# Score products split 512 + 128 and 384 + 256 over the halves of TensorE's rows, in four PSUM banks

## The chip, the cores and the metric

The kernel runs on one core of a Trainium2 chip. The core has TensorE (PE, with its weight loads as PEld), VectorE (DVE), ScalarE (ACT), GpSimd (POOL) and SyncE (SP, which here issues the DMAs). Matmuls write PSUM, which has eight banks of 512 fp32 columns by 128 partitions; VectorE and ScalarE read them from there. The metric is the device time of one execution in microseconds, as the median of several runs.

## The reference

The input x has 2048 rows of 576. One half of the work is causal attention over segments of 512 rows with 32 heads of 18 columns, together with a memory that is carried over the segments. The other is a feed-forward net with a gate over 4608 hidden columns. A gate per row mixes both.

```python
for s in range(N):                       # N = 4 segments of L = 512 rows
    qs, ks, vs = q[:, :, s], k[:, :, s], v[:, :, s]
    logits = jnp.einsum("bhqd,bhkd->bhqk", qs, ks) * scale + mask
    p = _softmax(logits, axis=-1)
    a_dot = jnp.einsum("bhqk,bhkd->bhqd", p, vs)
    ...
    o = g * a_mem + (1.0 - g) * a_dot
...
b = (_gelu(x @ w_gate) * (x @ w_up)) @ w_down
return g * a + (1 - g) * b
```

## The kernel before

Products are made of fp16 pairs (a high and a low part), so that a product of two fp32 operands takes three matmuls. After a first stage (projections, memory; about 230 us) the kernel runs 72 steps, `step(v)`, each of which forms the hidden columns of the feed-forward net for one tile of 128 hidden columns and half of the rows. Into most steps two further kinds of work are woven: the attention of one head for two segments, and the down products of the block of hidden columns before. The last stage multiplies by the output weights.

Four engines (PE, ACT, DVE, POOL) run their instructions in the order in which the code emits them; this order is written out by hand in `step`. SyncE's queue is not held to it.

**The row halves.** A head has 18 columns. Its queries and keys lie as three parts of 18 (54 rows), once at partitions 0 to 53 and once, copied, at partitions 64 to 117. So a score product takes 54 of the 128 rows of TensorE and can use either half of them. In `scores(a)` a segment of a head has four score products, one for each block of 128 queries (`qi` 0 to 3); causality leaves (qi + 1) x 128 key columns. `PIECES` says at which partition (0 or 64) each one reads, and in which order they are issued. Before, 512 columns (qi 3) are at 0, 384 and 128 (qi 2 and 0) at 64 in one bank, and 256 (qi 1) at 0.

**The banks.** `bank(tag, bufs)` takes one of the PSUM buffers of a tag. Tags G, U, V and pv have one bank each, st and dn two, which are taken in turn. The down chains take dn: `down` runs six matmuls (L999) and one VectorE instruction that adds the result to `acc` (L1007, in the first block L1005). Here dn is also taken by the score product of 256 columns, the others take st. Once in four steps a sum for the scales takes a dn bank as well.

**The evictions.** `scores` gives back a function `piece(i)`; `put(a, i)` calls it in a later place. It makes VectorE read a score bank, add the mask and write the logits to `pf` with their maximum (L910, a custom instruction and one that reads the accumulator).

**A step**, with k = v - 2 the head: `end_pair` finishes the hidden columns of the step before (`hidden`, L1021: VectorE scales what lies in G and U). The matmuls of this step fill V, G and U (L1039, L1046), with copies between them on VectorE (L1141, L1144, L1176). Between them stand single down chains (`early`, five a step). Then come `low_rests` (L1051, two matmuls of 64 rows), `scores(2k)` (the middle group), the additions of Y and V to the tiles g1 and g0 on VectorE (L1195, L1203; Y is the tile of bank U, X that of G), the values products of a segment before (`values`, L954, bank pv), two more chains, the last product into U, three chains (`late`), `low_rests` again, and `scores(2k + 1)` (the end group). The next step's first matmul goes to V. Segment 2k is evicted within the step, segment 2k + 1 at the start of the next. In one step of four, VectorE writes the result of four heads (`result_low`, L983) between the late chains' additions.

Of the kernel before, what the change touches and what calls it, by code (L numbers as in the profile page):

```python
# [13 lines left out]
OP = mybir.AluOpType  # L14
# [4 lines left out]
P = 128  # L19
# [3 lines left out]
DH = 18  # L23
L = 512
# [18 lines left out]
def kernel(ctx: ExitStack, tc: tile.TileContext, xs, wqk, wv, wo, wgu, wd, beta, out):  # L43
    nc = tc.nc
    pe, act, dve, pool, sp = nc.tensor, nc.scalar, nc.vector, nc.gpsimd, nc.sync
# [6 lines left out]
    def bank(tag, bufs=1, dt=F32):  # L52
        return ps.tile([P, 512 if dt == F32 else 1024], dt, name=tag, tag=tag, bufs=bufs)
# [255 lines left out]
    def low_d(f):  # L309
        t = pair_d[f]  # L310
        pool.tensor_tensor(t[:, 1], raw_d.pop(f), t[:, 0], OP.subtract)  # L311
# [67 lines left out]
    mask = cst.tile([P, L], BF16, name="mask")  # L379
# [16 lines left out]
    with tc.tile_pool(name="prj", bufs=2, side="right", reuse_waits="tile") as pp:  # L396
# [204 lines left out]
        with tc.manual_schedule(engines=ORDERED):  # L601
# [3 lines left out]
            start = bank("G")  # L605
# [241 lines left out]
    with tc.tile_pool(name="keep", bufs=2, side="right", reuse_waits="tile") as kp, ExitStack() as tail:  # L847
        home.update(d=kp)
        turns.update(of=2)
        hp, qts, kts, vts, obs, mx, prob = {}, {}, {}, {}, {}, {}, {}  # L850
# [34 lines left out]

        COL = [0, P, 3 * P, 6 * P, 10 * P]

        PIECES = (((3,), 0), ((2, 0), 64), ((1,), 0))

        def scores(a):  # L890

            k, e = divmod(a, 2)
            q, kt = qts[k], kts[k]
            mx[a] = ap_.tile([P, 4], F32, name="mx", bufs=2)
            prob[a] = ap_.tile([P, 10 * P], F32, name="pf", bufs=2)
            put = []
            for qis, r in PIECES:
                o = bank("dn", 2) if qis == (1,) else bank("st", 2)
                spots, off, h = [], 0, slice(r, r + 3 * DH)
                for qi in qis:  # L900
                    n = (qi + 1) * P
                    pe.matmul(o[:, off : off + n], q[h, e * L + qi * P : e * L + (qi + 1) * P],  # L902
                              kt[h, e * L : e * L + n], start=True, stop=True)
                    spots.append((qi, o[:, off : off + n]))
                    off += n
                put.append(spots)

            def piece(i):
                for qi, ov in put[i]:
                    dve.tensor_tensor_reduce(prob[a][:, COL[qi] : COL[qi + 1]], ov, mask[:, L - (qi + 1) * P :],  # L910
                                             1.0, -3e38, OP.add, OP.max, mx[a][:, qi : qi + 1])

            return piece

# [103 lines left out]
        def hidden(f, c, o, t):  # L1018

            sc = scl[f // 2][0]  # L1020
            dve.scalar_tensor_tensor(t, o, sc[:, 6 + c : 7 + c], t, OP.mult, OP.mult)  # L1021

        def hidden_pair(f, c, t):
            hh = hp[f, c] = (kp if f % 2 else mp2).tile([P, 2, L], F16, name=f"hh{f % 2}", bufs=6 - 2 * (f % 2))
            act.activation(hh[:, 0], t, AF.Copy)  # L1025
            pool.tensor_tensor(hh[:, 1], t, hh[:, 0], OP.subtract)  # L1026

        def gelu(f, c, o, t):
            act.activation(t, o, AF.Gelu_apprx_tanh, scale=scl[f // 2][0][:, 2 + c : 3 + c])  # L1029
# [77 lines left out]

        ends, puts = [], {}

        def end_pair():  # L1110

            for g in ends:
                hidden(*g)
            for f, c, o, g in ends:
                hidden_pair(f, c, g)
            ends.clear()

        def step(v):
# [3 lines left out]
            c, e = 2 * p, 2 * p + 1  # L1122
            k = v - LAG
# [4 lines left out]
            put = lambda a, i: puts[a](i) if a in puts else None  # L1128

            done = (k - 5) // 4 if i4 == 3 and 0 <= (k - 5) // 4 < H // 2 else None  # L1130
            low = (k - 6) // 4 if i4 == 0 and 0 <= (k - 6) // 4 < H // 2 - 1 else None
            x1, x2_, t = x16[c], x16[e], xt[p]
            end_pair()
            if v == 3:
                high_g(2, 1)
                low_g(2, 1)
# [11 lines left out]
                scale_result()  # L1148
            some(fb - 1, early[:1])
            put(2 * k - 1, 1)  # L1150
            put(2 * k - 1, 2)
            puts.pop(2 * k - 1, None)
            if on(k - 2):
                values(2 * k - 3)
# [37 lines left out]
                low_rests(f, (V, G4, x1), (Y, G4, x2_))  # L1192
            if on(k):
                puts[2 * k] = scores(2 * k)
            dve.tensor_tensor(g1, Y, g1, OP.add)  # L1195
            gelu(f, e, g1, g1)
            if v == 3:
                for n in range(2):
                    high_d(n)
                    low_d(n)  # L1200
            put(2 * k, 2)
            if fb:
                dve.tensor_tensor(g0, V, g0, OP.add)  # L1203
                gelu(f, c, g0, g0)
# [32 lines left out]
            if on(k):  # L1237
                puts[2 * k + 1] = scores(2 * k + 1)
# [37 lines left out]
        with tc.manual_schedule(engines=ORDERED):  # L1276
            for v in range(2 * NF):
                step(v)

                if v == LAST:  # L1280
                    atn.close()
                    op_ = tail.enter_context(tc.tile_pool(name="outp", bufs=2, side="right", reuse_waits="tile"))
                if v >= LAST:
                    turned(2 * (v - LAST))
                    turned(2 * (v - LAST) + 1)
                    finish(v - LAST)
            end_pair()
            turns.update(of=3)


            fb = NB - 1
            for t in range(10, 16):
                turned(t)
            for t in range(16):
                for n in range(2):
                    down(fb, t, n)
                for n in range(2):
                    o = bank("st", 2)
                    chain_x(o[:, :NH], lambda i: ot[t][:, i], lambda k, b: wos[k][:, b, n * NH : (n + 1) * NH])
                    av = acc[:, t, n * NH : (n + 1) * NH]  # L1300
                    dve.scalar_tensor_tensor(av, o[:, :NH], gate[:, 2, t : t + 1], av, OP.mult, OP.add)
                    if t == 15:
                        sp.dma_start(out[t * P :, n * NH : (n + 1) * NH], av)
                if t < 15:
                    sp.dma_start(out[t * P : (t + 1) * P, :], acc[:, t])
# [40 lines left out]
```

## Time and profile before

| | |
|---|---|
| median of 3 runs | 1612.19 us (1610.37 to 1613.04) |
| span of the profiled execution | 1608.8 us, granted TensorE clock 1.000 |
| the same execution outside its span | not listed; median less span is 3.4 us |
| DMA q1 | 206.92 MB, 71.1% of 16 engines |
| score products (L902) | 512 of 11924 matmuls, 259.3 to 1420.1 us |
| down products (L999) | 3396 matmuls into dn listed, 476.8 us, 286 ns each |
| score evictions (L910) from st | 183.9 us in 384 |
| additions of down products (L1007) | 274.0 us in 534, 516 ns each |

A row of the timeline gives start and length in us, engine, line, operation, what is written and read, tile shape and count; in brackets stands how long the engine was idle before and who ended that. Rows of equal instructions that follow each other are merged. The recorded length of a matmul is from its start to its modelled end, so matmuls overlap in the list. A row of groups gives the count, then busy us and mean ns of one, then the idle time before. A row of windows gives the stretch, its length, and for each engine busy us and count, then the granted clock, the DMA share and GB/s.

### The profile page before, as it was taken

What the parts mean: (1) busy time and instruction counts of PE and PEld (TensorE: products, weight loads), DVE (VectorE), ACT (ScalarE), POOL (GpSimd) and SP (SyncE); (2) the same over time, 40 slices, a digit from 0 to 9 for tenths busy, and PEclk for the clock granted to TensorE, in tenths of its full rate; (3) what the DMA queues carried; (4) which work ended last, traced back from release to release, by engine and by line L of the source; (5) the groups of instructions that cost most, each with busy time, mean ns of one, the idle gap of its engine ahead of it and who ended that gap; (6) DMA issues with size and microseconds to landing.
All of it is one profiled execution on the core that took longest, in us unless ns stands there. A gap on an engine that the chain in (4) does not pass through costs nothing.

```text
span 1608.8 us, 32608 instructions
## 1 busy us (share of the span) xinstructions
PE 1594.9 (99%) x11924; PEld 933.3 (58%) x11924; DVE 1141.2 (71%) x2938; ACT 1162.3 (72%) x1968; POOL 1132.9 (70%) x1093
## 2 busy tenths in 40 slices
PE   9999999999999999999999999999999999999999
PEld 6655754555555555555555555555555555555577
DVE  6575785677777777777777777777777777765543
ACT  6666446888888888888888888888888888863200
POOL 2233647798978888888978788887879787885200
PEclk9999999999999999999999999999999999999999
DMA  6532343788878788888987898878788797837251
GB/s 243 190 122 81 133 146 85 122 139 126 136 122 141 123 142 125 142 136 126 141 128 136 126 145 124 145 123 155 130 132 135 130 136 129 129 65 166 49 133 60
DMA packets 472016, 209.00 MB, mean 130 GB/s; under 512 B 427568, under 2 KB 437040, under 8 KB 471344
## 3 DMA queue, kind: packets, MB, share of 16 engines
q1 hardware_dynamic: 471856, 206.92, 71.1%
q8 instruction: 94, 1.54, 0.4%
q14 instruction: 66, 0.54, 0.1%
HBM read 90.99 MB, written 27.26 MB: 73 GB/s over the span
## 4 chain that ended last, share of the span: by engine, by line
PE 96%; DMA 1%; DVE 1%; POOL 1%; ACT 0%; issue 0%; SPq 0%; POOLq 0%; DVEq 0%
PE dn L999 26%; PE U L1039 17%; PE V L1039 12%; PE G L1039 11%; PE pv L954 4%; PE st L328 3%; PE st L318 3%; PE dn L328 2%; PE G L318 2%; PE U L1046 2%; PE st L902 2%; PE V L1051 1%; PE U L318 1%; PE G L1051 1%; PE V L1046 1%; PE G L1046 1%
## 5 line engine op out<-in xcount | busy, mean ns | idle before, releaser
L934 POOL TENSOR_TENSOR ph<-pf,ph 128x512 f16<-128x512 f32 (+1 forms) x256 | 354.0, 1404 | 177.8 <-ACT ph L933 175.9
L999 PE MATMUL dn<-paird,hh 128*128 128x288 f16 x3396 | 476.8, 286 | 0.9 <-POOL paird L311 0.9
L1039 PEld LDWEIGHTS <-pairg 128*128 128x128 f16 x3024 | 285.0, 98 | 312.6 <-issue 17.6
L999 PEld LDWEIGHTS <-hh 128*128 128x128 f16 x3456 | 332.3, 98 | 138.1 <-issue 2.6
L1007 DVE SCALAR_TENSOR_TENSOR acc<-dn,ev,acc 128x288 f32<-128x288 f32 x534 | 274.0, 516 | 95.9 <-PE dn L999 87.2
L923 ACT ACTIVATE pf<-pf,mb,esc 128x512 f32<-128x512 f32 (+3 forms) x512 | 292.9, 642 | 6.7
L1039 PE MATMUL G<-x,pairg 128*128 128x512 f16 x864 | 209.9, 379 | 4.0 <-DVE gl L1021 4.0
L1039 PE MATMUL U<-xt,pairg 128*128 128x512 f16 x864 | 210.0, 379 | 0.0
L1026 POOL TENSOR_TENSOR hh<-gl,hh 128x512 f16<-128x512 f32 x144 | 163.9, 1159 | 56.1 <-ACT hh L1025 56.1
L910 DVE CUSTOM_DVE_ANT_0 pf<-st,mask 128x512 f32<-128x512 f32 (+2 forms) x384 | 183.9, 504 | 0.0
L299 POOL TENSOR_TENSOR pairg<-raw,pairg 128x640 f16<-128x640 f32 (+2 forms) x144 | 173.9, 1230 | 10.6 <-ACT pairg L295 10.6
L933 ACT ACTIVATE ph<-pf 128x512 f16<-128x512 f32 (+1 forms) x256 | 172.4, 720 | 0.0
L1176 DVE COPY gl<-U 128x512 f32<-128x512 f32 x72 | 49.8, 691 | 135.6 <-PE U L1039 135.6
L295 ACT ACTIVATE pairg<-raw 128x640 f16<-128x640 f32 (+2 forms) x144 | 89.5, 648 | 69.9 <-POOL raw L289 40.7
L264 POOL TENSOR_SCALAR raw<-raw,sc 128x640 f32<-128x640 f32 x72 | 134.8, 1885 | 0.0
L1029 ACT ACTIVATE gl<-gl,sc 128x512 f32<-128x512 f32 x144 | 98.3, 717 | 45.9 <-DVE gl L1195 25.5
L1039 PE MATMUL V<-xt,pairg 128*128 128x512 f16 x432 | 105.7, 381 | 0.0
L1195 DVE TENSOR_TENSOR gl<-U,gl 128x512 f32<-128x512 f32 x72 | 49.7, 690 | 78.6 <-PE U L1051 71.3
L1039 PE MATMUL U<-x,pairg 128*128 128x512 f16 x432 | 105.0, 379 | 0.4 <-DVE gl L1195 0.4
L1039 PE MATMUL V<-x,pairg 128*128 128x512 f16 x432 | 104.8, 378 | 0.4 <-ACT hh L1025 0.2
L1025 ACT ACTIVATE hh<-gl 128x512 f16<-128x512 f32 x144 | 82.8, 616 | 24.9 <-DVE gl L1021 24.8
L920 ACT ACTIVATE mb<-mx,esc 128x4 f32<-128x4 f32 x128 | 37.8, 295 | 86.5 <-DVE mx L910 83.7
(268 smaller groups left out, 2566.6 us busy)
## 6 DMA issues: line engine op xcount, KB each, us to landing
raw<-in_wgu_dram SPq DMA_DIRECT2D x36, 640.0 KB
rawd<-in_wd_dram SPq DMA_DIRECT2D x36, 288.0 KB
qk<-stage SPq DMA_DIRECT2D x36, 256.0 KB
qt<-qk SPq DMA_DIRECT2D x128, 72.0 KB
kt<-qk SPq DMA_DIRECT2D x128, 72.0 KB
vp<-vstage SPq DMA_DIRECT2D x16, 296.0 KB
vt<-vp SPq DMA_DIRECT2D x16, 296.0 KB
qt<-qk SPq DMA_DIRECT2D x128, 36.0 KB
```

What stands on the lines that cost most here:

```text
L264: pool.tensor_scalar(r, r, scl[f // 2][0][:, 0:1], None, OP.mult)
L299: pool.tensor_tensor(spot(f, *p, 1), raw_g[f][:, p[0] : p[1]], spot(f, *p, 0), OP.subtract)
L318: pe.matmul(o, w(k, a), x[:, 4 * b + k], start=n == 0, stop=False)
L910: dve.tensor_tensor_reduce(prob[a][:, COL[qi] : COL[qi + 1]], ov, mask[:, L - (qi + 1) * P :], 1.0, -3e38, OP.add, OP.max, mx[a][:, qi : q ...
L923: act.activation(r, r, AF.Exp, bias=b[:, qi : qi + 1], scale=esc[:, 0, c : c + 1])
L933: act.activation(h[:, 0, cols], p[:, cols], AF.Copy)
L934: pool.tensor_tensor(h[:, 1, cols], p[:, cols], h[:, 0, cols], OP.subtract)
L999: pe.matmul(o[:, :NH], hh[:, a, q * P : (q + 1) * P], w[:, b, n * NH : (n + 1) * NH], start=i == 0, stop=i == 5)
L1007: dve.scalar_tensor_tensor(av, o[:, :NH], ev, av, OP.mult, OP.add)
L1026: pool.tensor_tensor(hh[:, 1], t, hh[:, 0], OP.subtract)
L1029: act.activation(t, o, AF.Gelu_apprx_tanh, scale=scl[f // 2][0][:, 2 + c : 3 + c])
L1039: pe.matmul(o, w[:, i, (a + k) * P : (a + k + 1) * P], x[:, b + k], start=start and k == 0 and i == 0 and b == h, stop=k == 1 and i == 1, ...
```

## The change

The four products are issued as 512 columns at partition 0, 384 at 64, 256 at 64 and 128 at 0. Each has a bank of its own: the first two in st, the last two in dn. `piece(i)` evicts one product. The two in dn are evicted first: for segment 2k directly behind the scores, ahead of the addition into g1; for segment 2k + 1 in the next step's `end_pair`, behind the scaling of G and ahead of that of U.

```diff
-        PIECES = (((3,), 0), ((2, 0), 64), ((1,), 0))
+        PIECES = ((3, 0), (2, 64), (1, 64), (0, 0))
...
-            for qis, r in PIECES:
-                o = bank("dn", 2) if qis == (1,) else bank("st", 2)
-                spots, off, h = [], 0, slice(r, r + 3 * DH)
-                for qi in qis:
-                    n = (qi + 1) * P
-                    pe.matmul(o[:, off : off + n], q[h, e * L + qi * P : e * L + (qi + 1) * P],
-                              kt[h, e * L : e * L + n], start=True, stop=True)
-                    spots.append((qi, o[:, off : off + n]))
-                    off += n
-                put.append(spots)
+            for i, (qi, r) in enumerate(PIECES):
+                h, n = slice(r, r + 3 * DH), (qi + 1) * P
+                o = bank("st" if i < 2 else "dn", 2)[:, :n]
+                pe.matmul(o, q[h, e * L + qi * P : e * L + (qi + 1) * P], kt[h, e * L : e * L + n],
+                          start=True, stop=True)
+                put.append((qi, o))
...
-        def end_pair():
+        def end_pair(between=()):
-            for g in ends:
+            for i, g in enumerate(ends):
                 hidden(*g)
+                if i == 0:
+                    for put in between:
+                        put()
...
-            end_pair()
+            end_pair([lambda i=i: put(2 * k - 1, i) for i in (2, 3)])
...
             put(2 * k - 1, 1)
-            put(2 * k - 1, 2)
...
                 puts[2 * k] = scores(2 * k)
+            put(2 * k, 2)
+            put(2 * k, 3)
             dve.tensor_tensor(g1, Y, g1, OP.add)
             gelu(f, e, g1, g1)
...
-            put(2 * k, 2)
```

The lines of the changed kernel stand up to five lower in number: the scores are L900 there, their evictions L906, the down chains L995, their additions L1003, `hidden` is L1017 and the next step's first product L1035.

TensorE at the end of a step, behind the late chains: the scores and the first matmul of the next step. Before, and then now, with the semaphores of the engines that each waits for:

```order
L902 LDWEIGHTS qt
L902 MATMUL st<-kt,qt 128x512
L902 LDWEIGHTS qt
L902 MATMUL st<-kt,qt 128x384
L902 LDWEIGHTS qt
L902 MATMUL st<-kt,qt 128x128
L902 LDWEIGHTS qt
L902 MATMUL dn<-kt,qt 128x256 [waits DVE_49]
L1039 LDWEIGHTS pairg
L1039 MATMUL V<-xt_2147,pairg 128x512
```

```order
L900 LDWEIGHTS qt
L900 MATMUL st<-kt,qt 128x512
L900 LDWEIGHTS qt
L900 MATMUL st<-kt,qt 128x384
L900 LDWEIGHTS qt
L900 MATMUL dn<-kt,qt 128x256 [waits DVE_49]
L900 LDWEIGHTS qt
L900 MATMUL dn<-kt,qt 128x128 [waits DVE_49]
L1035 LDWEIGHTS pairg
L1035 MATMUL V<-xt_2147,pairg 128x512
```

The product of 128 columns has moved to the end and into dn, and two of the four now wait for VectorE, where one did.

VectorE at the same place, from the additions of the late chains into the next step (ISA is the eviction of a score, first the custom instruction and then the reading of its accumulator). Before, and then now:

```order
L1007 SCALAR_TENSOR_TENSOR acc<-dn,ev,acc 128x288 [waits PE_49] x2
L1021 SCALAR_TENSOR_TENSOR gl<-G,sc,gl 128x512 [waits PE_49,Activation_49]
L1021 SCALAR_TENSOR_TENSOR gl<-U,sc,gl 128x512 [waits PE_49]
L1141 COPY gl<-V 128x512 [waits PE_49,Pool_49]
L910 ISA pf,mx<-st,mask 128x512 [waits Pool_49]
```

```order
L1003 SCALAR_TENSOR_TENSOR acc<-dn,ev,acc 128x288 [waits PE_49] x3
L1017 SCALAR_TENSOR_TENSOR gl<-G,sc,gl 128x512 [waits PE_49,Activation_49]
L906 ISA pf,mx<-dn,mask 128x256 [waits PE_49,Pool_49]
L906 ISA mx 128x1
L906 ISA pf,mx<-dn,mask 128x128 [waits PE_49]
L906 ISA mx 128x1
L1017 SCALAR_TENSOR_TENSOR gl<-U,sc,gl 128x512
L1140 COPY gl<-V 128x512 [waits PE_49]
L906 ISA pf,mx<-st,mask 128x512
```

The two evictions from dn have come between the scalings of G and U. (The first list is from a step in which L983 stands between the additions, so it shows two of three.)

VectorE in the middle of a step, from the addition of the last chain before the scores. Before, and then now:

```order
L1007 SCALAR_TENSOR_TENSOR acc<-dn,ev,acc 128x288 [waits PE_49]
L1195 TENSOR_TENSOR gl<-U,gl 128x512 [waits PE_49]
L910 ISA pf,mx<-dn,mask 128x256 [waits PE_49]
L910 ISA mx 128x1
L1203 TENSOR_TENSOR gl<-V,gl 128x512
```

```order
L1003 SCALAR_TENSOR_TENSOR acc<-dn,ev,acc 128x288 [waits PE_49]
L906 ISA pf,mx<-dn,mask 128x256 [waits PE_49]
L906 ISA mx 128x1
L906 ISA pf,mx<-dn,mask 128x128 [waits PE_49]
L906 ISA mx 128x1
L1195 TENSOR_TENSOR gl<-U,gl 128x512
L1202 TENSOR_TENSOR gl<-V,gl 128x512
```

Both evictions from dn now stand ahead of the addition of U.

More of the change, by code (lines that the diff above doesn't have):

```diff
@@ L896, in scores @@
             put = []
-            for qis, r in PIECES:
-                o = bank("dn", 2) if qis == (1,) else bank("st", 2)
-                spots, off, h = [], 0, slice(r, r + 3 * DH)
-                for qi in qis:
-                    n = (qi + 1) * P
-                    pe.matmul(o[:, off : off + n], q[h, e * L + qi * P : e * L + (qi + 1) * P],
-                              kt[h, e * L : e * L + n], start=True, stop=True)
-                    spots.append((qi, o[:, off : off + n]))
-                    off += n
-                put.append(spots)
+            for i, (qi, r) in enumerate(PIECES):
[4 more added lines that the diff above has]
+                put.append((qi, o))
             def piece(i):
-                for qi, ov in put[i]:
-                    dve.tensor_tensor_reduce(prob[a][:, COL[qi] : COL[qi + 1]], ov, mask[:, L - (qi + 1) * P :],
-                                             1.0, -3e38, OP.add, OP.max, mx[a][:, qi : qi + 1])
+                qi, ov = put[i]
+                dve.tensor_tensor_reduce(prob[a][:, COL[qi] : COL[qi + 1]], ov, mask[:, L - (qi + 1) * P :],
+                                         1.0, -3e38, OP.add, OP.max, mx[a][:, qi : qi + 1])
             return piece
```

## The prediction, on record before the changed kernel ran

> **What bounds the kernel now.** I read the page's busy times first, then the chain of work that ended last, then the busy times of one long stretch, and after that the timeline of TensorE and VectorE around a few score products.
>
> ```profile
> span 1608.8 us, 32608 instructions
> PE 1594.9 (99%) x11924; PEld 933.3 (58%) x11924; DVE 1141.2 (71%) x2938; ACT 1162.3 (72%) x1968; POOL 1132.9 (70%) x1093
> PE 96%; DMA 1%; DVE 1%; POOL 1%; ACT 0%; issue 0%; SPq 0%; POOLq 0%; DVEq 0%
> 300.00:1420.00 1120.00, 1120.00 (x8929) 639.71 (x8929) 845.58 (x2305) 942.09 (x1570) 940.71 (x866) 1.00 0.84 133
> ```
>
> The last row is the stretch in which the scores are computed: TensorE is busy for 1120.00 of 1120.00 us at a granted clock of 1.00, and VectorE for 845.58. So there TensorE's own sequence sets the time. What makes it shorter is gained and what makes it wait is lost, unless it waits already; the other engines matter only through the banks and tiles that they release.
>
> A step has two groups of four score products. The one in its middle, around 806.4:
>
> ```profile
> 806.16 0.39 PE L1051 MATMUL U<-x,pairg 64*128 64x512 f16 x1
> 806.38 0.38 PE L902 MATMUL st<-kt,qt 54*128 54x512 f16 x3
> 806.55 0.21 PE L902 MATMUL st<-kt,qt 54*128 54x128 f16 x1
> 806.60 0.27 PE L902 MATMUL dn<-kt,qt 54*128 54x256 f16 x1
> 806.80 0.67 PE L954 MATMUL pv<-vt,pt 128*128 128x37 f16 x20
> 807.32 0.65 PE L999 MATMUL dn<-paird,hh 128*128 128x288 f16 x4
> 806.59 0.69 DVE L1195 TENSOR_TENSOR gl<-U,gl 128x512 f32<-128x512 f32 x1 [1.32 <-PE U L1051]
> 807.20 0.41 DVE L910 CUSTOM_DVE_ANT_0 pf<-dn,mask 128x256 f32<-128x256 f32 x1
> 807.54 0.08 DVE L910 DVE_READ_ACCUMULATOR2_ANT mx<- 128x1 f32 x1
> L902 PE MATMUL st<-kt,qt 54*128 54x512 f16 x128 | 48.4, 378 | 0.0
> L902 PE MATMUL st<-kt,qt 54*128 54x384 f16 x128 | 41.5, 324 | 0.0
> L902 PE MATMUL dn<-kt,qt 54*128 54x256 f16 x128 | 34.2, 267 | 0.0
> L902 PE MATMUL st<-kt,qt 54*128 54x128 f16 x128 | 27.3, 213 | 0.0
> ```
>
> The row at 806.38 holds three products: 512 and 384 columns start together, on different halves of the rows, and 128 columns at 806.55, when the second half is through with its 384. The 256 columns start at 806.60, when the first half is through with its 512. The last four rows give the streaming time: 128 columns more cost 54 to 57 ns, so a product streams for about 55 ns for each 128 columns, and some 158 ns of its recorded time are the way through the array. The halves now stream 768 and 512 columns. From the start of the last product (806.60) to the next full-row matmul (806.80) are 0.20 us: 0.11 of streaming and 0.09 in which nothing starts.
>
> **Part 1: the even halves.** Afterwards the second half streams 384 and 256 columns, the first 512 and 128: 640 each. The 256 start at +0.17 (after the group's start) and have streamed at 0.28, the 128 start at +0.22 and have streamed at 0.275. Before, the last column was through at 0.33. That is **0.05 us less a group**, 128 groups, 6.4 us, if nothing waits. This part changes no weight load or eviction in number, and two evictions of one tile become evictions of two.
>
> **Part 2: the fourth product needs a second down bank.** The two dn banks are taken in turn by the down chains and the scores, so two score products in a row take both, and the second takes the bank that the last chain before it has just filled. At the end of a step three chains stand directly before the scores. The first and the last end group of the usual kind, each with the last chain's eviction, the last score product and the next step's first matmul (the last one's score product started at 1420.11 in the same way):
>
> ```profile
> 297.75 0.52 DVE L1005 TENSOR_SCALAR acc<-dn,ev 128x288 f32<-128x288 f32 x1 [0.25 <-PE dn L999]
> 298.09 0.27 PE L902 MATMUL dn<-kt,qt 54*128 54x256 f16 x1
> 298.29 0.39 PE L1039 MATMUL V<-xt,pairg 128*128 128x512 f16 x1
> 1419.77 0.52 DVE L1007 SCALAR_TENSOR_TENSOR acc<-dn,ev,acc 128x288 f32<-128x288 f32 x1 [0.25 <-PE dn L999]
> 1420.31 0.39 PE L1039 MATMUL V<-xt,pairg 128*128 128x512 f16 x1
> ```
>
> The last chain's eviction ends at 298.27, and the score product on dn started at 298.09, while that eviction ran: it had the other bank. Its successor in the turn gets the bank that is not free before 298.27. The fourth product now waits for that, on TensorE in order, with the whole next step queued behind it. How long TensorE takes to follow VectorE stands in a wait of the later part:
>
> ```profile
> 1510.72 0.74 DVE L1021 SCALAR_TENSOR_TENSOR gl<-G,sc,gl 128x512 f32<-128x512 f32 x1
> 1511.52 0.38 PE L1039 MATMUL G<-x,pairg 128*128 128x512 f16 x1 [1.00 <-DVE gl L1021]
> ```
>
> The first ends at 1511.46, the second starts 0.05 later. So the fourth starts at 298.32, has streamed at 298.375, and with the same 0.09 the next step starts at 298.47 instead of 298.29: **+0.18**. The gap of 0.09 I take as it stands, because it stands behind every group whatever its last product; its bounds are nothing, if the next weights are loaded during the wait, and 0.18, if the waiting group pays a change of rows twice.
>
> In one step of four, VectorE writes a head group's result (L983) between the evictions, and they end later. First and last of these:
>
> ```profile
> L983 DVE SCALAR_TENSOR_TENSOR oh<-ob,wsc,oh x16: 807/809/810, 370.3 to 1455.5; 128x576 f16<-128x576 f32 x16
> 370.98 0.93 DVE L1007 SCALAR_TENSOR_TENSOR acc<-dn,ev,acc 128x288 f32<-128x288 f32 x2
> 371.86 0.39 PE L1039 MATMUL V<-xt,pairg 128*128 128x512 f16 x1
> 1400.94 0.93 DVE L1007 SCALAR_TENSOR_TENSOR acc<-dn,ev,acc 128x288 f32<-128x288 f32 x2
> 1401.83 0.39 PE L1039 MATMUL V<-xt,pairg 128*128 128x512 f16 x1
> ```
>
> Evictions end at 371.91; plus 0.05, 0.055 and 0.09 is 372.11 against 371.86: **+0.25**. Of the sixteen results one (1455.5) comes after the last score, so 15 end groups are of this kind. The scores run over 64 steps, two of which have no down chains yet; 62 - 15 = 47 are of the usual kind. End groups: 47 x 0.18 + 15 x 0.25 = 8.5 + 3.8 = **12.2 us**.
>
> **Part 3: the middle groups.** There the chains before the scores were evicted long ago in most steps, so the four products run without a wait and the values products start 0.05 sooner. But the first down chain behind them now needs the bank of the 256 columns. VectorE takes these first: product ends 806.55 + 0.27 = 806.82, VectorE follows 0.04 later as at 806.59 (U's last product ends 806.55), needs 0.42 with the accumulator's reading (807.20 to 807.62), so 807.28, and 0.05 later the chain starts: 807.33, where it started at 807.32 before. The gain of 0.05 is gone, and about **0.015** lost. The second chain's bank is free 0.37 later, while the first chain streams for 0.73. In 8 of the 16 steps in which the block's scales are computed, by the timeline, the eviction before the middle group is late; the first and the last:
>
> ```profile
> 824.70 0.51 DVE L1007 SCALAR_TENSOR_TENSOR acc<-dn,ev,acc 128x288 f32<-128x288 f32 x1
> 825.29 0.37 PE L954 MATMUL pv<-vt,pt 128*128 128x37 f16 x8
> 1413.25 0.51 DVE L1007 SCALAR_TENSOR_TENSOR acc<-dn,ev,acc 128x288 f32<-128x288 f32 x1
> 1413.84 0.32 PE L954 MATMUL pv<-vt,pt 128*128 128x37 f16 x6
> ```
>
> 825.21 + 0.05 + 0.055 + 0.09 = 825.41 against 825.29: +0.12. Middle groups: 54 x 0.015 + 8 x 0.12 = **1.8 us**. The four groups of the two steps without chains keep their 0.05: **-0.2**.
>
> **Part 4: VectorE's new order, cost nothing.** In the middle the addition L1195 moves behind two evictions. It then ends at about 808.1 (two evictions until 807.6 or less, 0.69 after that, overlapped), and the next writer of its bank is
>
> ```profile
> 808.78 1.46 PE L1039 MATMUL U<-x,pairg 128*128 128x512 f16 x6
> 814.85 0.69 DVE L1141 COPY gl<-V 128x512 f32<-128x512 f32 x1 [0.21 <-PE V L1039]
> 816.08 0.70 DVE L1144 COPY U<-G 128x512 f32<-128x512 f32 x1
> 818.63 0.38 PE L1039 MATMUL U<-xt,pairg 128*128 128x512 f16 x1
> ```
>
> 0.6 us of cover. In the next step two evictions of 0.7 us together stand between the scalings of G and U; G's, for which TensorE's second product waits, stays first. The copy of G into U ends up to 0.6 later than 816.78, and U is written again at 818.63: 1.8 us of cover. If either cover failed, each 0.1 us beyond it would cost 6 us over 62 steps. SyncE's queue issues the same transfers, some turned pieces ahead of a load; the values use them a step later.
>
> **The skill against the rows.** The row: the next full-row matmul starts 0.09 behind the last streamed column of every score group. The Trainium skill (TensorE: Matmul & The Clock Gate, "Part 2: What happens when you issue a matmul") says that weight loads are pulled ahead of matmuls in flight, if their row groups don't conflict or a background buffer takes them. By this rule the 0.09 could vanish under the new wait; the rows don't show it at any of the groups. The Trainium skill (TensorEngine Tiling (Array Packing), "Key Properties") says that changing the tiling mode drains the engine, with which the 0.09 agrees; its section "PSUM Bottleneck" adds that tiling speeds up TensorE and not the evacuation, which is the forecast's direction.
>
> **The sum.** 12.2 + 1.8 - 0.2 = +13.8 us. The profiled execution has a span of 1608.8; the median of the runs is 1612.19, so 3.4 lie around it. 1608.8 + 13.8 + 3.4 = **1626.0 us**, +0.86%.
>
> **Rivals.**
> - *The next weights are loaded while the fourth product waits.* The 0.09 go at 62 end groups and 8 middle ones, 6.3 us: 1619.7. Against it: no group shows less than 0.09. Chance 0.11.
> - *The waiting group restarts more slowly*, as after a change of rows, another 0.09 at these 70: 1632.3. For it: the wait empties the array. Against it: product and weights of the waiting one are of the same mode. Chance 0.05.
> - *Not slower: the fourth product does not wait at the step's end.* It decides at an eviction that ends 0.17 after the group's start or earlier; it ends 0.40 after it now (298.27, group at 297.87 = 298.09 - 0.22). Then the end groups gain 62 x 0.05 = 3.1, and 1612.2 - 3.1 + 1.6 = 1610.7, no change; with the middle's waits gone too, 1612.2 - 6.4 = 1605.8. For it only that banks might be handed out otherwise than in turn; with two of them and two scores in a row there is no third. Chance 0.05 for the first and 0.04 for the second.
>
> The forecast itself has 0.75. Its rows are rounded to 0.01, so a term may be off by 0.03 a group, some 4 us over 124 groups; with the first rival and most of the second the range is 1619 to 1632. About 0.2% (3.2 us) is what a measurement of this kernel can tell from no change. Slower by more than that: 0.91; within it: 0.05; faster: 0.04.
>
> **What would show it.** In the changed profile a group's products start at 0, 0, +0.17 and, in the middle, +0.22 with the values at +0.37; at the end the fourth starts 0.05 behind the last chain's eviction, at about +0.45, and the next step at +0.60. Little of that is listed as idle time: the 256 columns' record lasts until +0.44. So TensorE's busy share stays near 99%, and the loss shows as start times and span alone. If the fourth product starts at +0.22 at the end too, part 2 is wrong; if next steps start 0.055 behind it, the gap was; if L1195 or the copy into U releases TensorE, part 4 was.

## The result, and the profile after

| | before | changed |
|---|---|---|
| median | 1612.62 us (1610.37 to 1613.13, 4 runs) | 1626.61 us (1624.46 to 1627.09, 4 runs) |
| ratio | | 1.0087, 95% interval 1.0072 to 1.0101 |
| span of the profiled execution | 1608.8 us | 1622.7 us |

The change makes the kernel slower by 14.0 us, 0.87%; the prediction was 1626.0. The page of the changed kernel, in the same lines as before (span; busy us with shares and counts; the chain that ended last, by engine):

```profile
span 1622.7 us, 32561 instructions
PE 1605.2 (99%) x11924; PEld 937.0 (58%) x11924; DVE 1130.4 (70%) x2938; ACT 1159.1 (71%) x1968; POOL 1132.8 (70%) x1093
PE 93%; DVE 3%; ACT 1%; DMA 1%; issue 1%; POOL 1%; SPq 0%; DVEq 0%; POOLq 0%
```

TensorE has the same 11924 matmuls and is still busy for 99% of the span. By busy time the loss looks like 10 us more work. Only the chain hints at the cause: VectorE's share of it has gone from 1% to 3%. The list of TensorE's waits (us in total, times, longest) doesn't name it either:

```profile
PE G L1035 <- DVE gl L1017: 4.0, 3, 2.7
PE pv L950 <- DMA pt<-ph: 3.2, 3, 1.5
PE U L1035 <- DVE gl L1195: 1.4, 1, 1.4
```

No score product stands there. (The last row, a wait behind L1195, was 0.4 us before; it is taken up under part 4 below.) The starts in the timeline show it. Two ends of a step, the first of the usual kind and the second with L979 (L983 before) between the additions, TensorE and VectorE (start, length; two products in a row where the count is x2):

```profile
799.48 0.52 DVE L1003 SCALAR_TENSOR_TENSOR acc<-dn,ev,acc 128x288 f32<-128x288 f32 x1 [0.22 <-PE dn L995]
800.25 0.52 DVE L1003 SCALAR_TENSOR_TENSOR acc<-dn,ev,acc 128x288 f32<-128x288 f32 x1 [0.25 <-PE dn L995]
800.37 0.38 PE L900 MATMUL st<-kt,qt 54*128 54x512 f16 x2
800.54 0.49 PE L900 MATMUL dn<-kt,qt 54*128 54x256 f16 x2
800.97 0.39 PE L1035 MATMUL V<-xt,pairg 128*128 128x512 f16 x1
...
818.47 0.93 DVE L1003 SCALAR_TENSOR_TENSOR acc<-dn,ev,acc 128x288 f32<-128x288 f32 x2
818.94 0.38 PE L900 MATMUL st<-kt,qt 54*128 54x512 f16 x2
819.11 0.56 PE L900 MATMUL dn<-kt,qt 54*128 54x256 f16 x2
819.61 0.39 PE L1035 MATMUL V<-xt,pairg 128*128 128x512 f16 x1
```

Counted from the group's start, the 256 columns start at +0.17 in both groups. The row that holds them and the 128 columns ends at 801.03; a product of 128 columns is recorded with 0.21, so it started at 800.82, +0.45, just 0.05 after the last chain's addition ended (800.77). The next step starts at +0.60 (800.97), in the second group at +0.67. Over the 62 end groups the next step's first matmul starts at +0.614 in the mean, at +0.419 before: 62 x 0.195 = 12.1 us. Almost none of it is idle time: in the first group the record of the 256 columns lasts until +0.44 and that of the 128 covers the rest. In the second, 0.08 lie between the two records (819.38 to 819.46), and the list of waits doesn't have them.

Step by step the loss is nowhere else. From 310 us to the last group, the distance to the next group's start has grown by 0.17 to 0.26 over every end group and by 0.02 to 0.08 over every middle one, 13.8 us in all; from the first matmul behind the last group to the end, both profiles take 188.5 us.

The middle of a step:

```profile
812.43 0.38 PE L900 MATMUL st<-kt,qt 54*128 54x512 f16 x2
812.60 0.27 PE L900 MATMUL dn<-kt,qt 54*128 54x256 f16 x2
812.80 0.67 PE L950 MATMUL pv<-vt,pt 128*128 128x37 f16 x20
813.40 0.41 PE L995 MATMUL dn<-paird,hh 128*128 128x288 f16 x2
812.91 0.42 DVE L906 CUSTOM_DVE_ANT_0 pf<-dn,mask 128x256 f32<-128x256 f32 x1 [1.60 <-PE dn L900]
813.26 0.08 DVE L906 DVE_READ_ACCUMULATOR2_ANT mx<- 128x1 f32 x1
813.47 0.69 DVE L1195 TENSOR_TENSOR gl<-U,gl 128x512 f32<-128x512 f32 x1
814.86 0.38 PE L1035 MATMUL U<-x,pairg 128*128 128x512 f16 x1
```

The values start at +0.37 instead of +0.42: here the even halves give their 0.05. The first chain starts at 813.40, +0.97, and had started at +0.94 (807.32). It follows the reading of the accumulator, which ends at 813.34. So the 0.05 are given back, with 0.03 more. The addition L1195 ends at 814.16, 0.7 ahead of the matmul that overwrites U (814.86).

### The profile page after: what moved, and what is told of

The parts are those of the page before. It is cut to its first block, busy times and chain, and to the rows that moved or that the text cites. A ratio compares the mean times of both kernels' runs of the same rounds, so it can differ in the third digit from the quotient of the medians.

```text
span 1622.7 us, 32561 instructions
## 1 busy us (share of the span) xinstructions
PE 1605.2 (99%) x11924; PEld 937.0 (58%) x11924; DVE 1130.4 (70%) x2938; ACT 1159.1 (71%) x1968; POOL 1132.8 (70%) x1093
## 4 chain that ended last, share of the span: by engine, by line
PE 93%; DVE 3%; ACT 1%; DMA 1%; issue 1%; POOL 1%; SPq 0%; DVEq 0%; POOLq 0%
PE dn L995 25%; PE U L1035 17%; PE V L1035 11%; PE G L1035 11%; PE pv L950 4%; PE st L328 3%; PE st L318 2%; PE U L1042 2%; PE dn L328 2%; PE dn L900 2%; PE G L318 1%; PE V L1047 1%; PE st L900 1%; PE G L1047 1%; PE G L1042 1%; PE V L1042 1%
## 5 line engine op out<-in xcount | busy, mean ns | idle before, releaser
L995 PE MATMUL dn<-paird,hh 128*128 128x288 f16 x3396 | 476.6, 286 | 0.3 <-POOL paird L311 0.3
L1035 PEld LDWEIGHTS <-pairg 128*128 128x128 f16 x3024 | 285.0, 98 | 324.7 <-issue 24.2
L995 PEld LDWEIGHTS <-hh 128*128 128x128 f16 x3456 | 335.9, 98 | 138.0 <-issue 1.9
L1003 DVE SCALAR_TENSOR_TENSOR acc<-dn,ev,acc 128x288 f32<-128x288 f32 x534 | 273.4, 515 | 87.3 <-PE dn L995 80.3
L1035 PE MATMUL G<-x,pairg 128*128 128x512 f16 x864 | 209.9, 379 | 4.0 <-DVE gl L1017 4.0
L1035 PE MATMUL U<-xt,pairg 128*128 128x512 f16 x864 | 210.0, 379 | 0.0
L906 DVE CUSTOM_DVE_ANT_0 pf<-st,mask 128x512 f32<-128x512 f32 (+1 forms) x256 | 156.9, 614 | 0.0
L906 DVE CUSTOM_DVE_ANT_0 pf<-dn,mask 128x256 f32<-128x256 f32 (+1 forms) x256 | 80.7, 353 | 84.2 <-PE dn L900 84.2
L1035 PE MATMUL U<-x,pairg 128*128 128x512 f16 x432 | 105.0, 379 | 1.4 <-DVE gl L1195 1.4
L1035 PE MATMUL V<-xt,pairg 128*128 128x512 f16 x432 | 105.7, 381 | 0.0
L1035 PE MATMUL V<-x,pairg 128*128 128x512 f16 x432 | 104.8, 378 | 0.7 <-DVE gl L1140 0.5
L950 PEld LDWEIGHTS <-pt 128*128 128x128 f16 x2560 | 78.3, 96 | 24.5 <-issue 17.0
```

Source lines behind the costliest of these rows:

```text
L950: pe.matmul(ov, pr[:, 10 * i + COL[qi] // P + kb], v[:, 4 * e + kb, c0 : c0 + VC], start=kb == 0 and i == 0, stop=kb == qi and i == 1)
L995: pe.matmul(o[:, :NH], hh[:, a, q * P : (q + 1) * P], w[:, b, n * NH : (n + 1) * NH], start=i == 0, stop=i == 5)
L1003: dve.scalar_tensor_tensor(av, o[:, :NH], ev, av, OP.mult, OP.add)
L1035: pe.matmul(o, w[:, i, (a + k) * P : (a + k + 1) * P], x[:, b + k], start=start and k == 0 and i == 0 and b == h, stop=k == 1 and i == 1, ...
```

## The experiments

Theory A is the prediction's: at the step's end the fourth score product waits for the bank of the last chain. Theory B puts the loss on VectorE's new order. Where no number of runs stands, it is 4 to 11. Each run of a group is compared with runs of the kernel before on the same chip.

**Two matmuls between the chains and the scores.** Nothing of the scores is changed; what stands ahead of them is. A product has six matmuls, and `only`, which is new, picks those that are issued.

```diff
-            product(Y, f, S4, x2_, 2, 6)
-            rest(Y, f, UG, x2_, (0,) if fb else (0, 1))
+            product(Y, f, S4, x2_, 2, 6, only=range(5))
             some(fb - 1, late[:1])
             if low is not None:
                 result_low(low)
             some(fb - 1, late[1:])
+            product(Y, f, S4, x2_, 2, 6, only=range(5, 6))
+            rest(Y, f, UG, x2_, (0,) if fb else (0, 1))
```

> The changed kernel, with two matmuls of the last product into U (its sixth, and the one of the rest) moved from ahead of the three late chains to behind them; the number of matmuls is the same. Theory A (the fourth score product at the step's end waits for the last chain's eviction): 0.43 us of other matmuls now stand between that chain and the scores, so its eviction ends 0.03 us ahead of the group's start, or 0.04 behind it in the steps with L983, and the fourth starts at +0.22 instead of +0.45 or +0.53. The next step starts at +0.37 instead of +0.614 in the mean: 62 x 0.244 = 15.1 us, so 1626.6 - 15.1 = 1611.5. Theory B (the loss comes from VectorE, whose two score evictions delay the scaling of U and the addition of U): nothing of that is changed, 1626 +- 1.5.

Measured: 1611.74 us (11 runs) beside 1612.31 (27), ratio 0.9998, interval 0.9989 to 1.0007. The loss is gone as far as the interval can tell. The step's end in its timeline:

```profile
795.58 0.52 DVE L1003 SCALAR_TENSOR_TENSOR acc<-dn,ev,acc 128x288 f32<-128x288 f32 x1 [0.25 <-PE dn L995]
796.13 0.38 PE L900 MATMUL st<-kt,qt 54*128 54x512 f16 x2
796.30 0.27 PE L900 MATMUL dn<-kt,qt 54*128 54x256 f16 x2
796.50 0.39 PE L1037 MATMUL V<-xt,pairg 128*128 128x512 f16 x1
```

The addition ends at 796.10, ahead of the group, and the next step starts at +0.37, as in all 62 end groups. VectorE's order is that of the change, so theory B falls. (The end groups now gain their 0.05 each; in the middle groups the chain still starts at +0.97.)

**One matmul alone.** The same with `range(6)` and no second part of the product, so that only `rest` stands behind the chains.

> The changed kernel with one matmul alone (the rest of U, 0.213 us) moved behind the late chains. Theory A: the eviction ends at 0.397 - 0.213 = +0.184 (47 groups) or 0.472 - 0.213 = +0.259 (15), the fourth starts at +0.237 or +0.312 and the next step at +0.383 or +0.458, 0.213 earlier in all 62: 13.2 us, 1613.4. Every 10 ns between chain and scores are then worth 10 ns. Theory B: 1626 +- 1.5.

Measured: 1614.71 us, ratio 1.0014, interval 1.0005 to 1.0023; which is 1613.1 to 1616.0 us and takes in the expectation of 1613.4. The timeline has the dose as expected:

```profile
796.77 0.52 DVE L1003 SCALAR_TENSOR_TENSOR acc<-dn,ev,acc 128x288 f32<-128x288 f32 x1 [0.25 <-PE dn L995]
797.11 0.38 PE L900 MATMUL st<-kt,qt 54*128 54x512 f16 x2
797.49 0.39 PE L1037 MATMUL V<-xt,pairg 128*128 128x512 f16 x1
```

The addition ends at +0.18, and the next step starts at +0.38. In this run and in the change, the fourth product of each of the 62 end groups starts 0.053 to 0.055 behind the end of that addition, whether this is at +0.18, +0.26, +0.40 or +0.47.

**The control.** The same move of two matmuls in the kernel before.

> The kernel before, with the same two matmuls moved behind the late chains. A control: there no score product waits for the last chain, so theory A expects nothing, 1612.3 +- 1. If the move were a gain by itself (of some 15 us, as in the changed kernel), it would be no test of the wait: 1597.

Measured: 1612.18 us beside 1611.92, ratio 1.0, interval 0.9991 to 1.0009. The move is no gain by itself; it gains where there is a wait to fill.

**VectorE's order alone**, in the kernel before (with `end_pair` as in the change):

```diff
-            end_pair()
+            end_pair([lambda: put(2 * k - 1, 2)])
...
-            put(2 * k - 1, 2)
...
                 puts[2 * k] = scores(2 * k)
+            put(2 * k, 2)
             dve.tensor_tensor(g1, Y, g1, OP.add)
...
-            put(2 * k, 2)
```

> The kernel before (its three banks and its uneven halves) with the eviction of its one dn score bank moved to the changed kernel's places: directly behind the middle scores ahead of the addition of U, and between the scalings of G and U in the next step. The prediction priced VectorE's new order at nothing (covers of 0.6 and 1.8 us): 1612.6. Theory B would show it here as a loss of some 10 us: 1622.

Measured: 1611.83 us, ratio 1.0001, interval 0.9992 to 1.001. The new places of one eviction cost nothing that the interval could show, where the prediction had said so. It moves one eviction and not the two of the change.

**The middle group's banks exchanged**, in the changed kernel (`e` is 0 for the segment of the middle group):

```diff
+            banks = [bank("st" if i < 2 else "dn", 2) for i in range(4)]
+            if e == 0:
+                banks[2:] = banks[:1:-1]
...
-                o = bank("st" if i < 2 else "dn", 2)[:, :n]
+                o = banks[i][:, :n]
...
-            put(2 * k, 2)
             put(2 * k, 3)
+            put(2 * k, 2)
```

> The changed kernel, with the banks of the two last score products of the middle group exchanged and their evictions too: the 128 columns are evicted first and have the bank that the first down chain behind the scores takes. The prediction has that chain wait for the 256 columns' eviction (0.42 us from +0.48, chain at +0.966 measured against +0.887 without a wait). Now 0.29 from +0.47, so 0.78, and the chain at +0.888: 54 x 0.08 = 4.3 us gained. In the 8 steps with a late eviction ahead of the group the 256 columns wait in place of the 128, 0.05 lost each. 1626.6 - 3.9 = 1622.7. If the chain is not held by that eviction: 1626.6.

Measured: 1623.12 us, ratio 1.0074, interval 1.0061 to 1.0087: 3.5 us less than the change by the medians and 2.1 by the ratios, each to its own runs of before. The two intervals overlap, so that the groups' timeline has to tell it:

```profile
811.26 0.38 PE L903 MATMUL st<-kt,qt 54*128 54x512 f16 x2
812.15 0.41 PE L998 MATMUL dn<-paird,hh 128*128 128x288 f16 x2
811.78 0.29 DVE L909 CUSTOM_DVE_ANT_0 pf<-dn,mask 128x128 f32<-128x128 f32 x1 [1.63 <-PE dn L903]
```

The first chain starts at +0.89, not +0.97, so that in the change it was held by the eviction of 256 columns.

**The banks with the old halves**, in the changed kernel:

```diff
-        PIECES = ((3, 0), (2, 64), (1, 64), (0, 0))
+        PIECES = ((3, 0), (2, 64), (0, 64), (1, 0))
```

> The changed kernel with the halves of before (512 and 256 columns at partition 0, 384 and 128 at 64), in the four banks and with the evictions of the change; the two last products change places, so that the 256 columns come last and wait. It prices the banks alone. By theory A the 256 start at +0.45 or +0.525, stream 0.11 instead of 0.055, and the next step starts at +0.65 or +0.73, +0.23 or +0.305 against before: 47 x 0.23 + 15 x 0.305 = 15.4. Middle groups start the values at +0.42 as before, and the first chain finds the bank of the 128 free: 0; 8 late ones +0.16 each = 1.3. 1612.3 + 16.7 = 1629.0, 2 to 3 us slower than the change. If the time that follows a wait did not depend on the last product's columns: 1626.

Measured: 1627.52 us, ratio 1.0098, interval 1.0084 to 1.0112. By time it isn't told apart from the change, since the intervals overlap. By the timeline it is:

```profile
783.38 0.52 DVE L1003 SCALAR_TENSOR_TENSOR acc<-dn,ev,acc 128x288 f32<-128x288 f32 x1 [0.25 <-PE dn L995]
783.51 0.38 PE L900 MATMUL st<-kt,qt 54*128 54x512 f16 x2
784.15 0.39 PE L1035 MATMUL V<-xt,pairg 128*128 128x512 f16 x1
```

The addition ends at 783.90 and the next step starts 0.25 later; in the change it is 0.20 (800.77 to 800.97). What streams behind the wait is paid in full: with the prediction's 0.055 for each 128 columns it is 0.11 against 0.055, and 0.09 and 0.05 stand around it in both.

**Both edits together**, two matmuls behind the chains and the middle's banks exchanged:

> The changed kernel with both edits of before: two matmuls of the last product into U behind the late chains, and the 128 columns of the middle group in the bank that the next chain takes and evicted first. Theory A, by the groups: 62 end groups without a wait, -0.05 each against the kernel before = -3.1; 54 middle groups whose next chain starts at +0.888 instead of +0.937, -2.7; 8 middle groups that wait for a late eviction with 256 columns last, +0.16 each = +1.3; four without chains, -0.2. 1612.3 - 4.7 = 1607.6, about 0.3% faster than the kernel before. If the gain of the even halves were hidden anyway: 1612.3.

Measured: 1606.85 us (6 runs) beside 1611.92 (16), ratio 0.9969, interval 0.9956 to 0.9981. This is faster than the kernel before by 5.1 us, where 4.7 were expected: with both waits gone, the gain of the even halves comes through. A middle group of it, and its waits between 300 and 1420 us:

```profile
805.91 0.38 PE L903 MATMUL st<-kt,qt 54*128 54x512 f16 x2
806.28 0.67 PE L953 MATMUL pv<-vt,pt 128*128 128x37 f16 x20
806.79 0.28 PE L998 MATMUL dn<-paird,hh 128*128 128x288 f16 x1
PE pv L953 <- DMA pt<-ph: 2.0, 2, 1.3
```

The values start at +0.37 and the chain at +0.88, some 0.05 sooner than before the change. The last row is a part of the gain that this execution loses again: twice TensorE waits for a transfer that the values need, 2.0 us in all, where the profile of before has no wait in this stretch.

Not tried: even halves in three banks, with the 128 columns behind the 384 in one bank. The two come from different halves of the rows, and nothing in the program would order their writes to that bank; whether that would work, no run here shows.

## Why the prediction was right, step by step

- **Part 1, 0.05 us a group: right.** Values start at +0.37 instead of +0.42. The 0.05 reach the total only where nothing waits behind them; in the change that is so at three of the four groups without chains.
- **Part 2, the wait at the step's end: right, and shown.** Forecast were +0.18 and +0.25 a group, 12.2 us; measured are 0.195 in the mean, 12.1 us. Filling the wait with 0.21 and 0.43 us of other matmuls took the loss away in that measure, and the same move without the wait gained nothing.
- **Part 3, the middle groups: the right total from two terms off.** A usual group was to lose 0.015; it lost 0.03, since the chain starts at +0.97 and not at +0.95 (the eviction with its reading ends at +0.915 and not at +0.897, and the release takes 0.055). Late evictions ahead of the group hold up 10 groups and not 8, but their chains lose 0.04 to 0.08 and not 0.12, since their chain stands behind VectorE's eviction in either case and the late one ends earlier now (+0.25 to +0.30, +0.31 to +0.34 before). Together the first chain starts 0.032 later in the mean of 62 groups, 2.0 us where 1.8 were forecast. That the total came out is in part luck: one term was too small and the other too large.
- **Part 4, VectorE's order at nothing: right in the sum, and wrong in one step.** The covers were 0.7 us (814.16 to 814.86) and over 1.8, and one eviction in the new places left the time as it was. But the prediction's own sign of being wrong, that L1195 releases TensorE, does occur once, in an early step in which the next product into U follows the scores directly; there was a short wait before, too. That product and the start of a later group, before and then now:

```profile
271.99 1.45 PE L1039 MATMUL U<-x,pairg 128*128 128x512 f16 x6 [0.36 <-DVE gl L1195]
288.71 0.38 PE L902 MATMUL st<-kt,qt 54*128 54x512 f16 x3
```

```profile
272.94 1.46 PE L1035 MATMUL U<-x,pairg 128*128 128x512 f16 x6 [1.45 <-DVE gl L1195]
288.60 0.38 PE L900 MATMUL st<-kt,qt 54*128 54x512 f16 x2
```

TensorE waits 1.45 us there and not 0.36. By 288.6 the changed kernel is level again, since TensorE's next waits, for GpSimd and for transfers, have become shorter. So the wait costs nothing in the end; the prediction hadn't looked at this step.

- **The sum: the 3.4 us around the span were wrong in kind.** In runs for which time and span are both listed, 1.7 to 1.8 us lie around the span. So the profiled execution of before took some 1610.6 us and was among the quickest, and the rest of the 3.4 is scatter. It does no harm, since it only turns a sum of spans into one of medians. The two profiled spans, both at a clock of 1.000, differ by 13.9 us, where 13.8 were forecast.
- **The rivals.** The next weights were not loaded during the wait: 0.15 lie between the start of the waiting 128 columns and the next step (800.82 to 800.97), as computed with 0.09. The same 0.15 says that the restart was not slower. The weight loads of the second end group shown above:

```profile
818.72 0.41 PEld L900 LDWEIGHTS <-qt 54*128 54x128 f16 x4
819.60 0.11 PEld L1035 LDWEIGHTS <-pairg 128*128 128x128 f16 x2 [0.47 <-issue]
```

The four loads of the scores, that of the waiting product too, have ended by 819.13, 0.33 ahead of its start; the next step's first load starts at 819.60, together with its matmul. It is so in all 62 end groups. The Trainium skill (TensorE: Matmul & The Clock Gate, "Part 2: What happens when you issue a matmul") has a load pulled ahead of matmuls in flight when the row groups don't conflict or when it goes to the background weight buffer. The full-row load shares its rows with the waiting product, so only the second way was open, and the trace shows that it wasn't taken here. The prediction took the 0.09 to agree with a drain of the engine. The trace leaves that open: the next matmul starts at 819.61, before the last product's modelled end at 819.67.

## What to carry to other kernels

When work is given one more buffer of a ring that another chain of work uses, look at who used that buffer last and how long ago: here the gain of 0.05 us a group was sure, and the bank cost 0.2, as it had been filled just before. The wait can be filled by moving independent work of the same engine in between, which cost nothing here, and the dose needed can be read from the timeline (0.23 us here, 0.30 in the steps in which VectorE writes a result). On a TensorE that is always busy by its records, look for such a loss in the distances between starts, not in idle time.

## What was not expected of the hardware

In seven of the nine profiled executions the granted clock fell to about half for some us, early in the steps, where TensorE idles for 2.3 us in two pieces because the values wait for a transfer. First the wait in the timeline of the run with two matmuls behind the chains, with windows of 2 us behind it (stretch and length, then for PE, PEld, DVE, ACT and POOL the busy us with counts, then the clock), and then a window of the kernel before:

```profile
290.59 0.19 PE L950 MATMUL pv<-vt,pt 128*128 128x37 f16 x1 [1.36 <-DMA pt<-ph]
291.69 0.64 PE L950 MATMUL pv<-vt,pt 128*128 128x37 f16 x19 [0.91 <-DMA pt<-ph]
292.00:294.00 2.00, 2.00 (x26) 1.49 (x23) 0.89 (x2) 1.79 (x3) 2.00 (x2) 0.80 0.57 105
294.00:296.00 2.00, 2.00 (x7) 0.73 (x5) 1.23 (x5) 0.66 (x2) 1.00 (x2) 0.50 0.88 163
296.00:298.00 2.00, 2.00 (x14) 1.36 (x13) 0.52 (x1) 1.99 (x3) 0.00 (x0) 0.84 0.00 0
```

```profile
294.00:296.00 2.00, 2.00 (x13) 1.15 (x12) 1.50 (x7) 0.45 (x2) 0.87 (x2) 1.00 0.82 152
```

In the first the clock is 0.50 between 294 and 296 us, and 7 matmuls run where 13 run in the second. The three windows lack 0.20, 0.50 and 0.16 of 2 us each, 1.7 us in all. In the profiles of before and of the changed kernel the clock stays at 1.00, although TensorE idles there in the same place and as long (1.53 and 0.92 us, 1.48 and 0.90); so the idle time alone doesn't decide it, and what does stays open. Over the runs of the kernel before beside the experiments, those with a mean clock of 1.000 took 1609.9 to 1610.7 us and those with 0.997 took 1613.3 to 1613.6; in between the two don't go together closely (1613.9 us at 0.999), so it is a part of the scatter and not all of it. No experiment here changed that wait, and the comparison of the two spans above is free of it.
